# An 18-wide attention beside a recurrent layer: four heads in lockstep, scores in four row tiles, values in four column tiles, division between two 32x32 vector transposes

## The chip, the cores and the metric

The kernel runs on one core of a Trainium2 chip. The metric is the device time of one execution in microseconds (us). The core's engines work side by side, each through its own list of instructions in a fixed order: TensorE (PE; its weight loads are shown apart as PEld), VectorE (DVE), ScalarE (ACT), GpSimd (POOL) and SyncE (SP), which here only issues DMA transfers. The array of TensorE has 128 rows (the contraction) and 128 columns (the outputs). A matmul whose operands use fewer may be placed in a part of the array, a tile of 32 rows or of 32 columns; the place is given in the code as `tile_position`.

## What is computed

Two layers on the same input of 2048 tokens by 576, mixed by a gate per token:

```python
g = _sigmoid((x * gate_w).sum(-1, keepdims=True))
a = _A_ref(x, A_mem0, A_Wq, A_Wk, A_Wv, A_Wo, A_seg_len)
b = _B_ref(x, B_wqkv, B_wo)
return g * a + (1 - g) * b
```

Layer A is recurrent. It goes through 64 segments of 32 tokens; each has 32 heads of 128, its 32 tokens stand behind 8 memory rows (40 positions in all), and the first 8 rows of a segment's output are the memory of the next. Layer B is plain attention over all 2048 tokens with 32 heads that are only 18 wide (`Dh = 576 // 32`):

```python
scores = jnp.einsum('bhqd,bhkd->bhqk', q, k) * scale
p = _softmax(scores, axis=-1)
o = jnp.einsum('bhqk,bhkd->bhqd', p, v)
```

## The kernel before

First x is transposed and layer B's queries, keys and values are projected into DRAM (`qtd`, `ktd`, `vgd`), in 8 groups (`g`) of four heads (`j`); the 18 rows of head j lie at partitions 32j to 32j+17. Then layer A runs, segment by segment. One segment is, on PE: five transposes of the new tokens (`ptx`), the query projection of 160 matmuls of 40 columns (`pb` from `wq`), the value projection of 20 and 20 matmuls of 512 columns (`pvv`) with the 160 of the key projection between them (`pb` from `wk`), the scores (`psh`), the row sums (`psums`), the reciprocal of the sums spread out by a matmul (`psn` from `diag`, which DVE makes), the weighted values (`pso`), the output projection of 160 matmuls of 40 columns (`pbw`) and five transposes (`pto`). Below, "projection stretch" is the time from the end of `pbw` to the first `pb` of `wk`, "key stretch" from there to the first `psums`, and "softmax stretch" from there to the end of `pbw`.

Layer B is cut into steps by the generator `b_steps`, and `b_advance` takes some of them at the end of each segment. A step before is two key blocks of one head: two score matmuls with 18 rows into one tile `sb` of two PSUM banks, one exponential on ACT over both (`etb`, 1024 elements a partition), and two matmuls that add the weighted values into `ob`. `vgd` holds the head's 18 value columns and 18 columns of ones, so that `ob` has the sums of the exponentials in rows 32 to 49. After eight steps DVE takes the reciprocal of those 18 rows, multiplies, and `stage` goes to `otd`. There are 1152 steps, 18 a segment. `sb` has two buffers, `etb` two, `ob` one; `qtg`, `ktg` and `vgi`, a group's operands, have one each, so a new group's load waits for the last use of the old.

The order on each engine is settled when the program is built, by a scheduler that moves instructions between the two layers: a step that is written at the end of segment s is spread over segment s and s+1. Each engine then takes its list strictly in order, and a waiting instruction holds up what is behind it. At the end `fin` multiplies `otd` with the output weights `wop` and mixes both layers.

Of the kernel before, what the change touches and what calls it, by code (L numbers as in the profile page):

```python
# [8 lines left out]
FP32 = mybir.dt.float32  # L9
BF16 = mybir.dt.bfloat16  # L10
ACT = mybir.ActivationFunctionType
ALU = mybir.AluOpType
# [4 lines left out]
def kernel(  # L17
# [15 lines left out]
    nc = tc.nc  # L33
    P = nc.NUM_PARTITIONS

    B_, S, Dm = A_x.shape
# [8 lines left out]
    DhB = Dm // HB  # L45
# [11 lines left out]
    KBB = 2  # L57
# [28 lines left out]
    wop = const.tile([P, GB, Dm], BF16, name="wop")  # L86
# [5 lines left out]
    vgd = dpool.tile([GB, P, NKB * 200], BF16, name="vgd")  # L92
# [5 lines left out]
    def dma(out_ap, in_ap):  # L98
        eng = dma_engs[dma_i[0] % 2]
        dma_i[0] += 1  # L100
        eng.dma_start(out=out_ap, in_=in_ap)

    with ExitStack() as bctx:
# [8 lines left out]
        nc.vector.memset(wop[:], 0.0)  # L112
        wo_v = B_wo.rearrange("(g j e) d -> j e g d", j=4, e=DhB)
        for j in range(4):
            dma(wop[32 * j:32 * j + DhB, :, :], wo_v[j])
# [29 lines left out]
        for g in range(GB):  # L145
# [36 lines left out]
            vg = bwork.tile([P, NKB, 200], BF16, name="vg")  # L182
            nc.vector.memset(vg[:], 0.0)
            nc.vector.memset(vg[:, :, :].rearrange("p k (j e) -> p k j e", e=50)[:, :, :, 32:50], 1.0)
            for kb in range(NKB):
                pv = ps_pj.tile([P, QC], FP32, name="pq")
                for c in range(NC):
                    cz = csz[c]
                    nc.tensor.matmul(
                        pv[:, 0:4 * DhB],  # L190
                        lhsT=xT[0:cz, c, kb * P:(kb + 1) * P],
                        rhs=wvg[0:cz, c, :],
                        start=(c == 0),
                        stop=(c == NC - 1),
                    )
                nc.any.tensor_copy(
                    out=vg[:, kb, :].rearrange("p (j e) -> p j e", e=50)[:, :, 0:DhB],
                    in_=pv[:, 0:4 * DhB].rearrange("p (j e) -> p j e", e=DhB),
                )
# [23 lines left out]
    bint2 = actx.enter_context(tc.tile_pool(name="bint2", bufs=2))  # L223
# [21 lines left out]
    nb_total = [0]  # L245

    def b_steps():
        for g in range(GB):
            qtg = bint.tile([P, S], BF16, name="qtg")
            ktg = bint.tile([P, S], BF16, name="ktg")  # L250
            vg = bint.tile([P, NKB * 200 + P], BF16, name="vgi")
            nc.sync.dma_start(out=qtg[:, :], in_=qtd[g])
            nc.scalar.dma_start(out=ktg[:, :], in_=ktd[g])
            nc.gpsimd.memset(vg[:, NKB * 200:NKB * 200 + P], 0.0)
            nc.sync.dma_start(out=vg[:, 0:NKB * 200], in_=vgd[g])
            for j in range(4):
                for qc in range(NQC):
                    ob = ps_bo.tile([P, 512], FP32, name="ob")
                    for kb0 in range(0, NKB, KBB):
                        nb = min(KBB, NKB - kb0)  # L260
                        sb = ps_bs.tile([P, KBB, 512], FP32, name="sb")
                        for i in range(nb):
                            kb = kb0 + i
                            nc.tensor.matmul(  # L264
                                sb[:, i, 0:QC],
# [6 lines left out]
                        etb = bint2.tile([P, KBB, 512], BF16, name="etb")  # L272
                        nc.scalar.activation(  # L273
                            out=etb[:, 0:nb, 0:QC], in_=sb[:, 0:nb, 0:QC], func=ACT.Exp, scale=scale_b
                        )
                        for i in range(nb):
                            kb = kb0 + i
                            nc.tensor.matmul(  # L278
                                ob[:, 0:QC],
                                lhsT=vg[:, kb * 200 + 50 * j:kb * 200 + 50 * j + P],  # L280
                                rhs=etb[:, i, 0:QC],
                                start=(kb == 0),
                                stop=(kb == NKB - 1),
                            )
                        nb_total[0] += 1
                        yield
                    rtb = bint.tile([P, 512], FP32, name="rtb")
                    nc.vector.reciprocal(out=rtb[0:DhB, 0:QC], in_=ob[32:32 + DhB, 0:QC])  # L288
                    stage = bint.tile([P, 512], BF16, name="stage")
                    nc.gpsimd.memset(stage[32 * j:32 * j + 32, 0:QC], 0.0)  # L290
                    nc.vector.tensor_tensor(
                        out=stage[32 * j:32 * j + DhB, 0:QC],
                        in0=ob[0:DhB, 0:QC],
                        in1=rtb[0:DhB, 0:QC],
                        op=ALU.mult,
                    )
                    nc.sync.dma_start(
                        out=otd[32 * j:32 * j + 32, g, qc * QC:(qc + 1) * QC],
                        in_=stage[32 * j:32 * j + 32, 0:QC],
                    )  # L300
                    yield

# [12 lines left out]

    total_steps = GB * 4 * NQC * ((NKB + KBB - 1) // KBB + 1)

# [198 lines left out]
    ps_f = ctx.enter_context(tc.tile_pool(name="ps_f", bufs=2, space=bass.MemoryType.PSUM))  # L516
    for n in range(NT):
# [33 lines left out]
#: Inputs that are plain numbers.  # L551
# [29 lines left out]
```

## Time and profile before

| | |
|---|---|
| median of 3 runs | 3421.55 us (3415.63 to 3444.35) |
| span of the profiled execution | 3430.3 us |
| PE busy | 3212.1 us, 94% |
| PEld / ACT / DVE / POOL busy | 1838.2 / 1518.2 / 1264.7 / 101.7 us |
| mean granted TensorE clock | 0.865 of full |

The profiled execution has no other time of its own than its span, which is 8.8 us above the median of the three runs. A busy PE in these tables is one with a matmul under way; matmuls overlap, so what a matmul costs is read from the distance between starts, not from its duration. The granted clock is 1.0 (2.4 GHz) or 0.5 (1.2 GHz) at any moment, and a mean of both over a stretch.

### The profile page before, as it was taken

What the parts mean: (1) busy time and instruction counts of PE and PEld (TensorE: products, weight loads), DVE (VectorE), ACT (ScalarE), POOL (GpSimd) and SP (SyncE); (2) the same over time, 40 slices, a digit from 0 to 9 for tenths busy, and PEclk for the clock granted to TensorE, in tenths of its full rate; (3) what the DMA queues carried; (4) which work ended last, traced back from release to release, by engine and by line L of the source; (5) the groups of instructions that cost most, each with busy time, mean ns of one, the idle gap of its engine ahead of it and who ended that gap; (6) DMA issues with size and microseconds to landing.
All of it is one profiled execution on the core that took longest, in us unless ns stands there. A gap on an engine that the chain in (4) does not pass through costs nothing.

```text
span 3430.3 us, 102385 instructions
## 1 busy us (share of the span) xinstructions
PE 3212.1 (94%) x47335; PEld 1838.2 (54%) x47765; DVE 1264.7 (37%) x1771; ACT 1518.2 (44%) x2227; POOL 101.7 (3%) x280
## 2 busy tenths in 40 slices
PE   5799999999999999999999999999999999999996
PEld 3445555555555555555555555555555555555553
DVE  5323433333333333333333433333433334333334
ACT  2334444444444444444444444444444444444440
POOL 0100000000000000000000000000000000000000
PEclk9868898898889888888988888898889888888988
DMA  5640000000000000000000000000000000000004
GB/s 122 191 170 5 4 5 27 4 4 5 5 26 5 5 5 26 5 5 4 5 27 5 4 5 5 26 5 5 5 26 5 5 5 4 27 5 5 5 5 106
DMA packets 92658, 78.36 MB, mean 23 GB/s; under 512 B 65212, under 2 KB 84356, under 8 KB 90500
## 3 DMA queue, kind: packets, MB, share of 16 engines
q1 hardware_dynamic: 62594, 52.33, 5.1%
q10 hardware_dynamic: 29634, 19.46, 2.2%
q8 instruction: 373, 6.11, 0.8%
q14 instruction: 57, 0.47, 0.0%
HBM read 47.90 MB, written 23.86 MB: 21 GB/s over the span
## 4 chain that ended last, share of the span: by engine, by line
PE 87%; issue 6%; DMA 3%; ACT 3%; DVE 1%; ACTq 0%; another core or an unknown queue 0%; DVEq 0%; SPq 0%; POOL 0%; POOLq 0%
PE pb L359 16%; PE pvv L379 16%; PE sb L264 16%; PE ob L278 14%; PE pbw L478 10%; PE psh L401 2%; PE psn L444 2%; PE psh L410 2%; PE pso L462 2%; ACT etb L273 2%; PE psums L425 2%; PE pq L170 1%; DMA ktg<-ktd 1%; PE pto L499 1%; DVE kt_sb L451 1%
## 5 line engine op out<-in xcount | busy, mean ns | idle before, releaser
L273 ACT ACTIVATE etb<-sb 128x1024 bf16<-128x1024 f32 x1024 | 1036.8, 1023 | 550.6 <-PE sb L264 290.5
L264 PE MATMUL sb<-qtg,ktg 18*128 18x512 bf16 x2048 | 710.3, 438 | 44.4 <-issue 17.8
L278 PE MATMUL ob<-etb,vgi 128*128 128x512 bf16 x1730 | 574.9, 405 | 36.3 <-ACT etb L273 18.2
L379 PE MATMUL pvv<-wv,ht 128*128 128x512 bf16 x2463 | 600.3, 380 | 5.4 <-issue 0.2
L288 DVE RECIPROCAL rtb<-ob 18x512 f32<-18x512 f32 x128 | 428.7, 3349 | 312.5 <-PE sb L264 286.9
L387 DVE CAST v_sb<-pvv 40x512 bf16<-40x512 f32 x256 | 174.8, 683 | 657.4 <-PE pvv L379 657.4
L379 PEld LDWEIGHTS <-ht 128*128 128x128 bf16 x2560 | 243.0, 98 | 296.5 <-issue 29.1
L359 PEld LDWEIGHTS <-wq 128*128 128x128 bf16 x10240 | 301.4, 98 | 164.7 <-issue 152.8
L478 PEld LDWEIGHTS <-wo 128*128 128x128 bf16 x10240 | 343.4, 110 | 39.5 <-issue 34.3
L389 ACT CAST v_sb<-pvv 40x512 bf16<-40x512 f32 x256 | 148.3, 579 | 487.3 <-PE pvv L379 487.3
L478 PE MATMUL pbw<-qt_sb,wo 128*128 128x40 bf16 x10240 | 349.6, 194 | 13.7 <-issue 13.6
L359 PE MATMUL pb<-ht,wq 128*128 128x40 bf16 x10240 | 331.4, 184 | 16.8 <-issue 16.4
L264 PEld LDWEIGHTS <-ktg 18*128 18x128 bf16 x2048 | 131.6, 98 | 340.9 <-issue 310.0
L278 PEld LDWEIGHTS <-vgi 128*128 128x128 bf16 x2048 | 156.2, 100 | 249.8 <-issue 198.2
L359 PEld LDWEIGHTS <-wk 128*128 128x128 bf16 x10240 | 268.6, 96 | 15.1
L359 PE MATMUL pb<-ht,wk 128*128 128x40 bf16 x10240 | 269.4, 180 | 0.0
L369 DVE CAST kt_sb<-pb 128x320 bf16<-128x320 f32 x128 | 63.0, 492 | 252.8 <-PE pb L359 252.8
L444 PEld LDWEIGHTS <-ones 40*40 40x40 bf16 x2048 | 81.3, 112 | 133.5 <-issue 125.3
L470 ACT CAST qt_sb<-pso 128x320 bf16<-128x320 f32 x128 | 54.5, 426 | 214.1 <-PE pso L462 214.1
L490 DVE CAST ht<-pbw 128x32 bf16<-128x32 f32 x63 | 12.1, 192 | 330.3 <-PE pbw L478 330.3
L432 DVE RECIPROCAL rq<-psums 40x32 f32<-40x32 f32 x64 | 22.4, 350 | 289.7 <-PE psums L425 289.7
L417 ACT ACTIVATE kt_sb<-psh 40x320 bf16<-40x320 f32 x256 | 110.4, 431 | 39.7 <-PE psh L410 16.1
(81 smaller groups left out, 1897.8 us busy)
## 6 DMA issues: line engine op xcount, KB each, us to landing
vgd<-vg ACTq DMA_DIRECT2D x8, 800.0 KB, 3.8
vgi<-vgd SPq DMA_DIRECT2D x8, 800.0 KB, 5.9
wo<-in_A_Wo_dram SPq DMA_DIRECT2D x1, 4608.0 KB, 54.2
qtd<-stg SPq DMA_DIRECT2D x8, 512.0 KB, 4.0
ktd<-stg SPq DMA_DIRECT2D x8, 512.0 KB, 4.8
qtg<-qtd SPq DMA_DIRECT2D x8, 512.0 KB, 5.1
ktg<-ktd ACTq DMA_DIRECT2D x8, 512.0 KB, 5.2
wq<-in_A_Wq_dram SPq DMA_DIRECT2D x1, 4096.0 KB
```

The costliest lines, as they stand in the source:

```text
L264: nc.tensor.matmul(sb[:, i, 0:QC], lhsT=ktg[32 * j:32 * j + DhB, kb * P:(kb + 1) * P], rhs=qtg[32 * j:32 * j + DhB, qc * QC:(qc + 1) * QC] ...
L273: nc.scalar.activation(out=etb[:, 0:nb, 0:QC], in_=sb[:, 0:nb, 0:QC], func=ACT.Exp, scale=scale_b)
L278: nc.tensor.matmul(ob[:, 0:QC], lhsT=vg[:, kb * 200 + 50 * j:kb * 200 + 50 * j + P], rhs=etb[:, i, 0:QC], start=(kb == 0), stop=(kb == NKB ...
L288: nc.vector.reciprocal(out=rtb[0:DhB, 0:QC], in_=ob[32:32 + DhB, 0:QC])
L359: nc.tensor.matmul(pb[:, 64 * j:64 * j + L], lhsT=w_tile[0:cz, c, h * Dh:(h + 1) * Dh], rhs=ht[0:cz, c, :], start=(c == 0), stop=(c == NC ...
L379: nc.tensor.matmul(ph[:, 0:512], lhsT=ht_flat[0:cz, L * c:L * c + P], rhs=wv[0:cz, c, q8 * qcols:(q8 + 1) * qcols], start=(c == 0), stop=( ...
L387: nc.vector.tensor_copy(out=v_sb[0:L, q8 * qcols:(q8 + 1) * qcols], in_=ph[0:L, :])
L389: nc.scalar.copy(out=v_sb[0:L, q8 * qcols:(q8 + 1) * qcols], in_=ph[0:L, :])
L401: nc.tensor.matmul(psh[0:L, 0:512], lhsT=ident[0:L, 0:L], rhs=mb8[0:L, :], start=True, stop=False,)
L417: nc.scalar.activation(out=vw(et[0:L, HS * h0:HS * (h0 + 8)], HS, L), in_=vw(psh[0:L, :], 64, L), func=ACT.Exp, scale=scale_a,)
L444: nc.tensor.matmul(psn[0:L, 64 * j:64 * j + L], lhsT=ones[0:L, 0:L], rhs=diag3[0:L, L * h:L * (h + 1)], start=True, stop=True,)
L478: nc.tensor.matmul(pbwv[0:cz, c, 0:L], lhsT=wo[:, h, c * P:c * P + cz], rhs=ot_sb[:, HS * h:HS * h + L], start=(h == 0), stop=(h == H - 1),)
```

## The change

Layer B's four heads of a group now go together. A step is one key block of four heads: four score matmuls, one in each 32-row tile of the array, into two `sb` tiles; two exponentials; and four value matmuls with 32 output columns each, one in each 32-column tile of the array, into the four quarters of one `ob`. `vgd` has 32 columns a head: 18 values, one column of ones, 13 of zeros. After sixteen steps DVE turns `ob` over in blocks of 32 by 32, takes the reciprocal of one column per block, multiplies, and turns the result back. There are 512 steps, 8 a segment. `etb` gets a third buffer, the load of `ktg` moves from ACT's queue to SP's, and `wop` is loaded behind layer A instead of at the start.

```diff
-            for j in range(4):
-                for qc in range(NQC):
-                    ob = ps_bo.tile([P, 512], FP32, name="ob")
-                    for kb0 in range(0, NKB, KBB):
...
+            for qc in range(NQC):
+                ob = ps_bo.tile([P, QC], FP32, name="ob")
+                for kb in range(NKB):
+                    sbs = []
+                    for jp in range(2):
+                        sb = ps_bs.tile([P, 2, QC], FP32, name="sb")
+                        for i in range(2):
+                            j = 2 * jp + i
                             nc.tensor.matmul(
-                                sb[:, i, 0:QC],
+                                sb[:, i, :],
                                 lhsT=ktg[32 * j:32 * j + DhB, kb * P:(kb + 1) * P],
                                 rhs=qtg[32 * j:32 * j + DhB, qc * QC:(qc + 1) * QC],
...
                                 tile_position=(32 * j, 0),
                             )
...
-                            nc.tensor.matmul(
-                                ob[:, 0:QC],
-                                lhsT=vg[:, kb * 200 + 50 * j:kb * 200 + 50 * j + P],
-                                rhs=etb[:, i, 0:QC],
...
+                    for j in range(4):
+                        nc.tensor.matmul(
+                            ob[32 * j:32 * j + 32, :],
+                            lhsT=vg[:, kb * P + 32 * j:kb * P + 32 * j + 32],
+                            rhs=ets[j // 2][:, j % 2, :],
...
+                            tile_position=(0, 32 * j),
                         )
...
-                    nc.vector.reciprocal(out=rtb[0:DhB, 0:QC], in_=ob[32:32 + DhB, 0:QC])
...
+                nc.vector.transpose(out=tq[:, :, :].rearrange("p b e -> p (b e)"), in_=ob[:, :])
...
+                nc.vector.reciprocal(out=rtb[:, :, :], in_=tq[:, :, DhB:DhB + 1])
...
+                nc.vector.transpose(out=stage[:, :], in_=tn[:, :, :].rearrange("p b e -> p (b e)"))
```

What the scheduler makes of it on PE in the projection stretch of a segment in mid-run (a line of dots stands for the second instruction of a pair, or for more of the same). Before, two values of one head, two scores of one head, twice over, and then pieces of the query projection:

```order
L278 LDWEIGHTS vgi_22721
L278 MATMUL ob_27910<-etb_27949,vgi_22721 128x512
...
L264 LDWEIGHTS ktg_22720
L264 MATMUL sb_27960<-qtg_22719,ktg_22720 128x512
...
L278 MATMUL ob_27910<-etb_27956,vgi_22721 128x512
...
L264 MATMUL sb_27974<-qtg_22719,ktg_22720 128x512
...
L359 MATMUL pb_28033<-ht_27881,wq_1905 128x40
```

Now, in the same stretch of the same segment:

```order
L270 MATMUL ob_27630<-etb_27667,vgi_22496 32x512
...
L255 LDWEIGHTS ktg_22495
L255 MATMUL sb_27676<-qtg_22494,ktg_22495 128x512
...
L351 LDWEIGHTS wq_1899
L351 MATMUL pb_27739<-ht_27591,wq_1899 128x40
```

The four heads do not stand together: they come as two values, two scores, then 7 to 31 matmuls of the query projection, eight times a segment, then twice two values alone. The stretch opens with three values and four scores in a row. Before, one run of 91 `pb` stood without layer B; now the longest is 31. The 20 `pvv` that were partly mixed with layer B follow in one run.

On PE in the softmax stretch, around the last 8 of the 32 `psn`, before:

```order
L264 MATMUL sb_27925<-qtg_22719,ktg_22720 128x512
L264 MATMUL sb_27932<-qtg_22719,ktg_22720 128x512
...
L444 LDWEIGHTS ones_63
L444 MATMUL psn_27670<-diag3_1946,ones_63 40x40
...
L462 MATMUL pso_27680<-kt_sb_1944,v_sb_1945 128x40
```

Now:

```order
L255 MATMUL sb_27634<-qtg_22494,ktg_22495 128x512
L270 MATMUL ob_27630<-etb_27637,vgi_22496 32x512
L436 MATMUL psn_27380<-diag3_1940,ones_63 40x40
...
L255 MATMUL sb_27645<-qtg_22494,ktg_22495 128x512
L454 MATMUL pso_27390<-kt_sb_1938,v_sb_1939 128x40
...
L454 MATMUL pso_27400<-kt_sb_1938,v_sb_1939 128x40
...
L270 MATMUL ob_27630<-etb_27639,vgi_22496 32x512
```

Where three scores in a row stood ahead of the `psn` and nothing between the 32 `pso`, single scores and values of layer B now stand between pieces of layer A. Over the whole softmax stretch of an even segment the order before was 24 `psums`, 2 scores, 8 `psums`, 2 scores, 2 values, 3 scores, 24 `psn`, 3 scores, 8 `psn`, 32 `pso`, 24 `pbw`, 2 values, 136 `pbw`; it is now 24 `psums`, 2 scores, 8 `psums`, 2 scores, 2 values, 2 scores, 2 values, 1 score, 24 `psn`, 1 score, 8 `psn`, 1 value, 8 `pso`, 1 value, 1 score, 8 `pso`, 2 values, 1 score, 16 `pso`, 16 `pbw`, 2 scores, 1 value, 144 `pbw`. An odd segment differs from it by a few places. In every eighth segment, where a group of heads ends, layer B stands out of the way from the `psn` to the end of `pbw`.

On DVE between `diag` and the memory rows of the next segment (`ht`), before, which stood so once a segment, with a second division in the projection stretch:

```order
L433 TENSOR_TENSOR diag3_1946<-ident_58,rq_1947 40x1280
L288 RECIPROCAL rtb_17529<-ob_16734 18x512
L451 TENSOR_TENSOR kt_sb_1944<-psn_17265,kt_sb_1944 40x320
...
L472 CAST qt_sb_1943<-pso_17315 128x320
L291 TENSOR_TENSOR stage_17531<-ob_16734,rtb_17529 18x512
L472 CAST qt_sb_1943<-pso_17335 128x320
```

Now, in every second segment, and none in the projection stretch:

```order
L425 TENSOR_TENSOR diag3_1940<-ident_58,rq_1941 40x1280
L281 STREAM_TRANSPOSE tq_27621<-ob_25920 128x512
L443 TENSOR_TENSOR kt_sb_1938<-psn_27350,kt_sb_1938 40x320
...
L283 RECIPROCAL rtb_27623<-tq_27621 128x16
L464 CAST qt_sb_1937<-pso_27400 128x320
L285 TENSOR_TENSOR tn_27625<-tq_27621,rtb_27623 128x512
L464 CAST qt_sb_1937<-pso_27420 128x320
L292 STREAM_TRANSPOSE stage_27627<-tn_27625 128x512
```

The first vector transpose has taken the place of the long reciprocal ahead of the four multiplications (`kt_sb` from `psn`) for which PE's `pso` wait; the rest of the division stands behind them.

## Rows read from the trace of the kernel before

**Rows 1.** The page: span, and busy time of each engine.
```profile
span 3430.3 us, 102385 instructions
PE 3212.1 (94%) x47335; PEld 1838.2 (54%) x47765; DVE 1264.7 (37%) x1771; ACT 1518.2 (44%) x2227; POOL 101.7 (3%) x280
```
**Rows 2.** Costliest groups: line, engine, operation xcount | busy us, mean ns | idle before.
```profile
L273 ACT ACTIVATE etb<-sb 128x1024 bf16<-128x1024 f32 x1024 | 1036.8, 1023 | 550.6 <-PE sb L264 290.5
...
L288 DVE RECIPROCAL rtb<-ob 18x512 f32<-18x512 f32 x128 | 428.7, 3349 | 312.5 <-PE sb L264 286.9
```
**Rows 3.** The last instructions of every segment: ns, first and last start in us.
```profile
L499 PEld LDWEIGHTS <-ots x320: 88/96/150, 236.7 to 3373.1; 128*32 128x32 bf16 x128, 64*32 64x32 bf16 x32
```
**Rows 4.** Stretches: limits, length, busy us (instructions), granted clock, DMA share, GB/s.
```profile
2522.45:2544.70 22.25, 21.92 (x237) 9.86 (x240) 7.31 (x11) 13.76 (x17) 0.52 (x1) 1.00 0.03 6
2544.70:2555.60 10.90, 10.85 (x216) 7.34 (x215) 2.35 (x4) 3.86 (x8) 0.33 (x2) 1.00 0.01 2
2506.83:2522.45 15.62, 13.78 (x271) 9.94 (x272) 8.59 (x11) 5.27 (x7) 0.52 (x1) 0.67 0.02 4
1079.00:1102.30 23.30, 22.83 (x237) 10.33 (x239) 7.36 (x11) 13.76 (x17) 0.52 (x1) 0.93 0.03 6
```
**Rows 5.** PE in order of time, projection stretch: start us, us, instruction, count.
```profile
2523.70 0.38 PE L264 MATMUL sb<-qtg,ktg 18*128 18x512 bf16 x1
2523.71 0.26 PE L344 MATMUL ptx<-ident,xseg 32*128 32x32 bf16 x4
...
2525.48 0.59 PE L278 MATMUL ob<-etb,vgi 128*128 128x512 bf16 x2
2526.00 0.60 PE L264 MATMUL sb<-qtg,ktg 18*128 18x512 bf16 x2
2526.53 0.62 PE L359 MATMUL pb<-ht,wq 128*128 128x40 bf16 x18
2527.00 0.59 PE L278 MATMUL ob<-etb,vgi 128*128 128x512 bf16 x2
```
**Rows 6.** The same place of another segment, where the scores work on partitions 0 to 17.
```profile
2575.58 0.60 PE L264 MATMUL sb<-qtg,ktg 18*128 18x512 bf16 x2
2576.02 0.25 PE L344 MATMUL ptx<-ident,xseg 32*128 32x32 bf16 x4
```
**Rows 7.** PE in order of time, first segment, at half clock.
```profile
176.81 1.03 PE L264 MATMUL sb<-qtg,ktg 18*128 18x512 bf16 x2
177.77 1.03 PE L278 MATMUL ob<-etb,vgi 128*128 128x512 bf16 x2
...
188.70 3.21 PE L359 MATMUL pb<-ht,wq 128*128 128x40 bf16 x91
191.74 1.32 PE L278 MATMUL ob<-etb,vgi 128*128 128x512 bf16 x3
```
**Rows 8.** Stretches as in rows 4: around that run, and around a fall.
```profile
175.30:188.70 13.40, 13.01 (x78) 3.59 (x80) 3.52 (x2) 5.12 (x5) 0.00 (x0) 0.50 1.01 425
188.70:192.40 3.70, 3.64 (x93) 3.31 (x94) 1.40 (x3) 0.43 (x1) 0.00 (x0) 0.50 1.01 427
192.40:202.00 9.60, 8.35 (x44) 2.46 (x43) 1.90 (x1) 8.40 (x9) 0.00 (x0) 1.00 1.06 390
1086.60:1090.00 3.40, 3.30 (x65) 1.97 (x66) 3.20 (x1) 1.50 (x3) 0.00 (x0) 1.00 0.00 0
1090.00:1093.50 3.50, 3.28 (x66) 2.38 (x64) 1.81 (x4) 0.84 (x2) 0.00 (x0) 0.51 0.07 16
```
**Rows 9.** PE in order of time, softmax stretch; in brackets the idle time before.
```profile
2514.25 0.42 PE L444 MATMUL psn<-diag,ones 40*40 40x40 bf16 x8 [0.96 <-DVE kt_sb L451]
...
2517.83 4.52 PE L478 MATMUL pbw<-qt_sb,wo 128*128 128x40 bf16 x136 [0.22 <-issue]
```
**Rows 10.** DVE groups as in rows 2, and a transfer with us to landing.
```profile
L387 DVE CAST v_sb<-pvv 40x512 bf16<-40x512 f32 x256 | 174.8, 683 | 657.4 <-PE pvv L379 657.4
...
ktg<-ktd ACTq DMA_DIRECT2D x8, 512.0 KB, 5.2
```

More of the change, by code (lines that the diff above doesn't have):

```diff
@@ L91 @@
     ktd = dpool.tile([GB, P, S], BF16, name="ktd")
-    vgd = dpool.tile([GB, P, NKB * 200], BF16, name="vgd")
+    vgd = dpool.tile([GB, P, NKB * P], BF16, name="vgd")
     otd = dpool.tile([P, GB, S], BF16, name="otd")
@@ L250, in b_steps @@
             ktg = bint.tile([P, S], BF16, name="ktg")
-            vg = bint.tile([P, NKB * 200 + P], BF16, name="vgi")
+            vg = bint.tile([P, NKB * P], BF16, name="vgi")
             nc.sync.dma_start(out=qtg[:, :], in_=qtd[g])
[L253 to L256, printed above, removed]
-                for qc in range(NQC):
-                    ob = ps_bo.tile([P, 512], FP32, name="ob")
-                    for kb0 in range(0, NKB, KBB):
[L260 to L263, printed above, removed]
+            nc.sync.dma_start(out=ktg[:, :], in_=ktd[g])
+            nc.sync.dma_start(out=vg[:, :], in_=vgd[g])
+            for qc in range(NQC):
[6 more added lines that the diff above has]
+                            j = 2 * jp + i
                             nc.tensor.matmul(
-                                sb[:, i, 0:QC],
+                                sb[:, i, :],
                                 lhsT=ktg[32 * j:32 * j + DhB, kb * P:(kb + 1) * P],
@@ L297, in b_steps @@
[L297 to L300, printed above, removed]
-                    yield
+                        sbs.append(sb)
+                    ets = []
+                    for jp in range(2):
+                        etb = bint3.tile([P, 2, QC], BF16, name="etb")
+                        nc.scalar.activation(out=etb[:, :, :], in_=sbs[jp][:, :, :], func=ACT.Exp, scale=scale_b)
+                        ets.append(etb)
@@ new lines, in b_steps @@
+                    for j in range(4):
[3 more added lines that the diff above has]
+                            rhs=ets[j // 2][:, j % 2, :],
+                            start=(kb == 0),
+                            stop=(kb == NKB - 1),
+                            tile_position=(0, 32 * j),
+                        )
+                    yield
+                tq = bint.tile([P, QC // 32, 32], FP32, name="tq")
@@ new lines, in b_steps @@
+                nc.vector.transpose(out=tq[:, :, :].rearrange("p b e -> p (b e)"), in_=ob[:, :])
+                rtb = bint.tile([P, QC // 32, 1], FP32, name="rtb")
+                nc.vector.reciprocal(out=rtb[:, :, :], in_=tq[:, :, DhB:DhB + 1])
+                tn = bint.tile([P, QC // 32, 32], BF16, name="tn")
+                nc.vector.tensor_tensor(
+                    out=tn[:, :, :],
+                    in0=tq[:, :, :],
+                    in1=rtb[:, :, :].to_broadcast([P, QC // 32, 32]),
+                    op=ALU.mult,
+                )
@@ L303 @@
+                stage = bint.tile([P, QC], BF16, name="stage")
+                nc.vector.transpose(out=stage[:, :], in_=tn[:, :, :].rearrange("p b e -> p (b e)"))
+                nc.sync.dma_start(out=otd[:, g, qc * QC:(qc + 1) * QC], in_=stage[:, :])
     bgen = b_steps()
@@ L516 @@
     ps_f = ctx.enter_context(tc.tile_pool(name="ps_f", bufs=2, space=bass.MemoryType.PSUM))
+    finc = ctx.enter_context(tc.tile_pool(name="finc", bufs=1))
+    wop = finc.tile([P, GB, Dm], BF16, name="wop")
+    nc.vector.memset(wop[:], 0.0)
+    wo_v = B_wo.rearrange("(g j e) d -> j e g d", j=4, e=DhB)
+    for j in range(4):
+        dma(wop[32 * j:32 * j + DhB, :, :], wo_v[j])
     for n in range(NT):
```

35 lines of the change are left out of this document (5 added, 30 removed).

## The prediction

> **What bounds the kernel now.** Read the page's busy times first: PE is under way for 94% of the span, no other engine for half of it [rows 1]. The mean segment, from the last instructions of the first to those of the 64th, is (3373.1 - 236.7) / 63 = 49.8 us [rows 3], so 64 segments are nearly the whole span and the change has to be read in one of them. The stretches of one segment say where its time lies: 22.25 us in the projection stretch, 10.90 in the key stretch, 15.62 in the softmax stretch, 48.8 together [rows 4]. In the first two PE is busy to within 0.4 us, ACT for 13.76 of 22.25 us: PE's own list is the bound there, not the exponentials, whose 1024 times 1.02 us [rows 2] are 16.4 us a segment. In the softmax stretch PE has 1.8 us of gaps; 0.96 of them is the wait for a multiplication on DVE [rows 9], ahead of which DVE's list has a 3.35 us reciprocal [rows 2].
>
> The clock is the second thing to see. It is full in the first two stretches and at a mean of 0.67 in the softmax stretch; in another segment it also falls within the projection stretch, which then takes 23.30 us instead of 22.25 [rows 4].
>
> **Prices.** At full clock a pair of scores or of values is 0.53 us from start to start (2525.48, 2526.00, 2526.53), and 18 `pb` take 0.47 us, 0.026 each [rows 5]. At half clock a pair is 0.96 us and 91 `pb` take 3.04 us, 0.033 each [rows 7]. So half clock costs narrow work a quarter, wide work nearly double.
>
> Do tiles overlap? The trace of before has a natural test. The scores of head j use rows 32j to 32j+17, `ptx` uses rows 0 to 31. Where j is not 0, `ptx` starts 0.01 us after a score that takes at least 0.21 us to stream [rows 5]; where j is 0 it starts 0.44 us after the first of two scores [rows 6], when both are through. Two row tiles run at once. A pair in two row tiles then saves one streaming (512 columns: 0.213 us at 2.4 GHz, 0.427 at 1.2), less 0.01 and a little for the loads: I take 0.31 us at full clock and 0.56 at half. The Trainium skill (TensorE: Matmul & The Clock Gate, Part 3) gives 3.07 times for four row tiles; the trace agrees in kind [rows 5, 6]. For column tiles no row of before has two: the bounds are 0.31 (overlap like rows) and 0.53 us (one after the other). I take 0.31, the mechanism being the same array cut the other way, and keep 0.53 as a rival. The same section gives 2.38 times for three column tiles, by which a pair would also come out near the lower bound.
>
> A rule speaks against the change. The row first: two values plus two scores at full clock cost 1.05 us where four streamings make 0.85 [rows 5], so each change of shape costs 0.10 us, and by the same working 0.11 at half clock [rows 7]; going from `pb` to values did not (18 `pb` at 2526.53, values at 2527.00, 0.026 us apiece [rows 5]), and to column tiles it will: ten times 0.10 us in a projection stretch. The Trainium skill (TensorEngine Tiling (Array Packing), Key Properties) states that changing the tiling mode drains the engine; by that rule too the gain is less than the tiles promise.
>
> **The change, part by part.** By the order, four tiles seldom stand together: layer B's 32 scores and 32 values of a segment come as some 35 groups, mostly pairs. That halves the streaming, it does not quarter it.
>
> *Projection stretch, full clock throughout.* 20 groups (three values, four scores, ten pairs of values, eight of scores) at 0.31 = 6.2; 160 `pb` at 0.026 = 4.1; 20 `pvv` at 0.213 = 4.3; ten entries into column tiles 1.0; `pto` and `ptx` 0.8: 16.4 us. Then waits: ten exponentials at 1.03 in a row from 0.9 us on end at 11.5 or so, the last two pairs of values wait for them, and behind stand 16 to 22 `pb` and the `pvv`: about 0.9 us more, 17.3 in all, against 22.25.
>
> *Projection stretch at half clock* from 2.5 us after its start: 2.5 + 17 groups at 0.56 (9.5) + 160 `pb` at 0.033 (5.3) + ten entries at 0.11 (1.1) + `pvv`. In the first segment the clock came back at 192.40, after 3.7 us of the unbroken run of `pb` and values from 188.70 [rows 7, 8]; so I let some eleven `pvv` (4.7 us) run at 0.427 and nine at 0.213: 6.6. Sum 25.0 us.
>
> *Key stretch:* nothing of layer B in it before or now, 10.9.
>
> *Softmax stretch.* Before, 10 scores and 4 values stood in it; now 12 and 9, in 14 groups, half of them single, which save nothing, and mostly at half clock. Going down the new list from the first `psums`: last 8 `psums` at 1.0, first pair of values at 2.2 (it waits for its exponential), second at 3.25, `psn` at 4.4, last 8 `psn` at 5.8, `pso` from 6.8 to 10.5, 16 `pbw`, two scores, one value, 144 `pbw` from 12.4 at 0.033 to 17.1. Against 15.62 that loses 1.5 us, although the 0.96 us behind the reciprocal are gone.
>
> *DVE.* Two divisions a segment, each 3.35 us of reciprocal [rows 2] and more, become one per two segments of two transposes, a 16-element reciprocal and a multiplication. No row has a transpose; the bounds are 0.68 us (a cast of 512 from PSUM [rows 10]) and 3.35 (the 512-element reciprocal [rows 2]). I take 0.68. It is then over before the first `psn` is through, and costs nothing; at 3.35 it would put about 2 us before the `pso` of every second segment, 64 us over the run. I keep 64 for the upper end.
>
> *The rest.* ACT: the same 1024 exponentials. `ktg` on SP's queue stands behind `qtg`, 5.2 us to land [rows 10]; it is due while 160 `pbw` (5 us) and 32 `psn` and `pso` run, so it costs nothing, 5 us for each of seven groups if that cover went. `wop` behind layer A waits for a memset and a load like that, beside the first `otn`: about 4 us at the end. It removes as little at the start.
>
> **Sum.** A segment is 17.3 + 10.9 + 17.1 = 45.3 us where the clock holds in the projection stretch and 25.0 + 10.9 + 17.1 = 53.0 where it does not. The mean now is 49.8. So all hangs on the share of segments in which it falls; at 4.5 / 7.7 = 0.58 of them nothing is gained.
>
> What did PE do when it fell? Between 1086.60 and 1090.00 PE was busy 3.30 of 3.40 us, with 18-row scores and `pb`, hardly any value matmul, and the clock was at half right after [rows 8]. From 175.30 to 188.70 it stayed at half with PE busy 13.01 of 13.40 us on alternating pairs with 8 to 23 `pb` between [rows 8]. So a busy PE does not hold the clock; work that fills little of the array lets it go, and short pieces do not fetch it back. The change does just this: values fill 64 columns at a time instead of 128, no run of `pb` exceeds 31, and the first 2 us of the projection stretch hold seven tile matmuls, the ten small transposes and a wait. At the other end the `pbw`, in which the clock came back, are cut by two scores and a value. Against it: in mid-stretch `pb` now stand in every gap, 40 full columns each 0.026 us, which held the clock in the key stretch's 160. I cannot work a share out of rows. I take 0.48, one segment in two: 45.3 + 0.48 x 7.7 = 49.0 us, 0.8 less than now, 64 times: -51 us, +4 at the end. From the span, 3430.3 - 47 = 3383; the span is 8.8 above the median of the runs, so about 3375.
>
> **Rivals.**
> *The clock holds* in all but 0.15 of the segments: 46.5 us, 64 x -3.3 = -211 + 4, from the median 3214. For it: the steady `pb`. The Trainium skill's page (TensorE: Matmul & The Clock Gate, Why this matters for your kernels) asks only that PE not stand idle; by that rule this rival would be what comes, for PE has no long gap; the trace bears that out badly [rows 8].
> *The clock is lost* in 0.9 of them: 52.2 us, 64 x 2.4 = +154 + 4, 3580: slower. It decides from 0.58 on. For it: PE's work around the fall and in the long half-clock stretch [rows 8].
> *Column tiles take turns:* 11 groups of values cost 0.22 more at full clock or 0.42 at half in the projection stretch, three pairs 0.4 in the softmax stretch: +4.8 us a segment on the likeliest, 53.8: 64 x 4.0 = +256 + 4, 3682. For it: no row shows column tiles together. Against: row tiles do overlap [rows 5, 6].
>
> **Chances.** About half the segments 0.37, with its own range of 3300 to 3470; clock held 0.20; clock lost 0.30; columns in turn 0.13. The range leaves out the lower half of the second and the upper part of the last two, with the transposes' bound of 64 us in it: 3210 to 3680. Within 1% (3387 to 3456) is about what a measurement of this kernel cannot tell from no change. Faster: 0.20 and half of the first case, 0.39. Same: about a third of the first and a little of the third, 0.15. Slower: the rest, 0.46.
>
> **What will show it.** Two scores of a pair, and two values, should start within 0.02 us of each other; if values start 0.21 apart, columns take turns. A pair at full clock should cost 0.31 us. The stretches of several segments should be 17 us at clock 1.0 or 25 near 0.5, and the share of each is the test of the sum. The softmax stretch should be longer than before, some 17 us. The transposes should be near 0.7 us and no `pso` wait for them. I am wrong in the mechanism if the projection stretch at full clock exceeds 19 us: then ACT or a wait bounds it.

## The result, and the profile after

The changed kernel takes 3174.55 us (median of 4 runs, 3170.39 to 3178.94) against 3422.87 us of the kernel before, beside which it ran: ratio 0.927, 95% interval 0.924 to 0.930. It is 7.3% faster. The prediction had said 3375 us, in a range from 3210 to 3680, with 0.39 for faster; the time lies below the range, nearest to the rival "the clock holds" (3214).

The page of the changed kernel, with the rows that answer to [rows 1] and [rows 2] (L267 is the exponential, L281 and L292 are the two transposes, L283 the reciprocal between them, L285 the multiplication):

```profile
span 3176.8 us, 101992 instructions
PE 3024.0 (95%) x47622; PEld 1807.9 (57%) x47765; DVE 813.6 (26%) x1664; ACT 1481.7 (47%) x2206; POOL 33.7 (1%) x144
...
L267 ACT ACTIVATE etb<-sb 128x1024 bf16<-128x1024 f32 x1024 | 1011.0, 1024 | 385.2 <-PE sb L255 370.3
```

From its groups by line, DVE's share of layer B:

```profile
L281 DVE STREAM_TRANSPOSE tq<-ob 128x512 f32<-128x512 f32 x32 | 22.9, 717 | 14.9 <-PE ob L270 14.9
L292 DVE STREAM_TRANSPOSE stage<-tn 128x512 bf16<-128x512 bf16 x32 | 22.5, 703 | 0.3
L285 DVE TENSOR_TENSOR tn<-tq,rtb 128x512 bf16<-128x512 f32 x32 | 21.8, 682 | 0.0
```

PE is still under way for 95% of a shorter span; DVE lost a third of its work: the divisions took 428.7 us of long reciprocals [rows 2] and 86.8 us of multiplications over the run, and the new ones take 75 us in all. A transpose costs 0.70 to 0.72 us.

The last instructions of every segment, as in [rows 3], give a mean segment of (3115.1 - 236.9) / 63 = 45.7 us instead of 49.8:

```profile
L491 PEld LDWEIGHTS <-ots x320: 88/96/97, 236.9 to 3115.1; 128*32 128x32 bf16 x128, 64*32 64x32 bf16 x32
```

63 x 4.1 = 258 us: the gain is all in the segments. In the mean over 63 segments, from the records of the trace, the projection stretch went from 22.9 to 18.5 us, the key stretch stayed at 11.0 and the softmax stretch went from 16.0 to 16.3. The clock has no part in this gain: over the span its mean fell from 0.865 to 0.826, and in the projection stretch from 0.97 to 0.92. What the tiles save by overlapping is more than what the clock takes back.

Stretches as in [rows 4] (projection, key and softmax stretch of a segment in mid-run, then the projection stretch behind the start of a group of heads, and two pieces of the softmax stretch ahead of that one):

```profile
2334.61:2351.68 17.07, 16.63 (x235) 9.23 (x234) 3.26 (x9) 11.15 (x15) 0.00 (x0) 1.00 0.03 8
2351.68:2362.60 10.92, 10.87 (x216) 7.36 (x215) 2.35 (x4) 3.86 (x8) 0.33 (x2) 1.00 0.01 2
2318.47:2334.55 16.08, 15.36 (x280) 9.99 (x277) 4.58 (x8) 7.10 (x9) 0.00 (x0) 0.68 0.01 2
2374.65:2403.16 28.51, 27.45 (x248) 11.47 (x247) 3.27 (x9) 15.67 (x19) 0.00 (x0) 0.58 0.01 4
2362.00:2366.30 4.30, 3.26 (x62) 2.00 (x59) 1.96 (x3) 2.80 (x4) 0.00 (x0) 1.00 0.21 62
2366.30:2373.00 6.70, 6.24 (x174) 5.91 (x171) 4.60 (x10) 0.85 (x2) 0.00 (x0) 0.50 0.59 217
```

A projection stretch with the clock held is 17.07 us, as predicted (17.3), and one that loses it, behind the start of a group, 28.51 here. But of 63 segments 50 hold the clock there and only 13 lose it: 7 in which the matmuls of a new group of heads stand, and 6 others. PE in order of time shows the pairs, at full clock in the first four rows and at half clock in the last three (as in [rows 5] and [rows 7]):

```profile
2336.51 0.39 PE L270 MATMUL ob<-etb,vgi 128*32 128x512 bf16 x2 [0.21 <-ACT etb L267]
2336.83 0.39 PE L255 MATMUL sb<-qtg,ktg 18*128 18x512 bf16 x2
2337.15 0.37 PE L351 MATMUL pb<-ht,wq 128*128 128x40 bf16 x8
2337.45 0.39 PE L270 MATMUL ob<-etb,vgi 128*32 128x512 bf16 x2
...
2384.66 0.61 PE L270 MATMUL ob<-etb,vgi 128*32 128x512 bf16 x2
2385.20 0.61 PE L255 MATMUL sb<-qtg,ktg 18*128 18x512 bf16 x2
2385.74 1.21 PE L351 MATMUL pb<-ht,wq 128*128 128x40 bf16 x31
```

Two values take 0.32 us from start to start (2336.51 to 2336.83) and two scores 0.32 (to 2337.15); at half clock 0.54. Both kinds of tile overlap.

### The profile page after: what moved, and what is told of

Read it like the earlier page. It is cut to its first block, busy times and chain, and to the rows that moved or that the text cites. A ratio compares the mean times of both kernels' runs of the same rounds, so it can differ in the third digit from the quotient of the medians.

```text
span 3176.8 us, 101992 instructions
## 1 busy us (share of the span) xinstructions
PE 3024.0 (95%) x47622; PEld 1807.9 (57%) x47765; DVE 813.6 (26%) x1664; ACT 1481.7 (47%) x2206; POOL 33.7 (1%) x144
## 4 chain that ended last, share of the span: by engine, by line
PE 88%; ACT 6%; DMA 3%; DVE 1%; issue 1%; ACTq 0%; SPq 0%; DVEq 0%
PE pb L351 19%; PE pvv L371 18%; PE ob L270 13%; PE sb L255 13%; PE pbw L470 11%; ACT etb L267 5%; PE pso L454 3%; PE psh L393 3%; PE psn L436 3%; PE psh L402 2%; PE pq L164 2%; PE psums L417 1%; DMA otn<-otd 1%; DMA wq<-in_A_Wq_dram 1%; PE po L525 1%
## 5 line engine op out<-in xcount | busy, mean ns | idle before, releaser
L267 ACT ACTIVATE etb<-sb 128x1024 bf16<-128x1024 f32 x1024 | 1011.0, 1024 | 385.2 <-PE sb L255 370.3
L270 PE MATMUL ob<-etb,vgi 128*32 128x512 bf16 x2048 | 527.3, 471 | 55.0 <-ACT etb L267 49.4
L255 PE MATMUL sb<-qtg,ktg 18*128 18x512 bf16 x2048 | 537.4, 465 | 0.0
L351 PE MATMUL pb<-ht,wq 128*128 128x40 bf16 x10240 | 382.2, 185 | 15.4 <-DMA wq<-in_A_Wq_dram 15.4
L255 PEld LDWEIGHTS <-ktg 18*128 18x128 bf16 x2048 | 106.9, 94 | 264.7 <-issue 255.7
L361 DVE CAST qt_sb<-pb 128x320 bf16<-128x320 f32 x128 | 62.9, 492 | 623.2 <-PE pb L351 617.4
L270 PEld LDWEIGHTS <-vgi 128*32 128x32 bf16 x2048 | 121.6, 95 | 168.9 <-issue 122.8
L443 DVE TENSOR_TENSOR kt_sb<-psn,kt_sb 40x320 bf16<-40x320 f32 x256 | 111.8, 475 | 73.1 <-PE psn L436 72.6
L454 PEld LDWEIGHTS <-v_sb 40*128 40x128 bf16 x2048 | 79.8, 107 | 75.9 <-issue 75.0
L363 ACT CAST kt_sb<-pb 128x320 bf16<-128x320 f32 x128 | 54.4, 425 | 129.9 <-PE pb L351 129.9
```

Of the source, the lines that this page charges most:

```text
L255: nc.tensor.matmul(sb[:, i, :], lhsT=ktg[32 * j:32 * j + DhB, kb * P:(kb + 1) * P], rhs=qtg[32 * j:32 * j + DhB, qc * QC:(qc + 1) * QC], s ...
L267: nc.scalar.activation(out=etb[:, :, :], in_=sbs[jp][:, :, :], func=ACT.Exp, scale=scale_b)
L270: nc.tensor.matmul(ob[32 * j:32 * j + 32, :], lhsT=vg[:, kb * P + 32 * j:kb * P + 32 * j + 32], rhs=ets[j // 2][:, j % 2, :], start=(kb == 0),
L351: nc.tensor.matmul(pb[:, 64 * j:64 * j + L], lhsT=w_tile[0:cz, c, h * Dh:(h + 1) * Dh], rhs=ht[0:cz, c, :], start=(c == 0), stop=(c == NC ...
L361: nc.vector.tensor_copy(out=dst, in_=src)
L443: nc.vector.tensor_tensor(out=vw(et[0:L, HS * h0:HS * (h0 + 8)], HS, L), in0=vw(psn[0:L, :], 64, L), in1=vw(et[0:L, HS * h0:HS * (h0 + 8)] ...
```

## The experiments

Theory A: the gain is the overlap of the tiles; without it the clock would be lost as well, because it falls where a busy PE works with little of its array. Theory B: the clock falls only where PE waits, and the gain is DVE's long reciprocals or the new order. In the table, "lost" counts the segments, of 63, whose mean granted clock between the output transposes and the first `pvv` is below 0.95, from the records of the trace; the mean segment is worked out as above.

| kernel | us | ratio to before (95%) | mean segment | lost |
|---|---|---|---|---|
| before | 3423 | 1 | 49.8 | 21, most for a few us alone |
| changed | 3175 | 0.927 (0.924-0.930) | 45.7 | 13 |
| no overlap | 4094 | 1.198 (1.190-1.206) | 60.2 | 57 |
| column tiles alone overlap | 3794 | 1.107 (1.104-1.110) | 55.2 | 44 |
| row tiles alone overlap, values full width | 3260 | 0.952 (0.950-0.954) | 47.0 | 9 |
| query projection with 64 rows | 3486 | 1.021 (1.015-1.026) | 50.5 | 63 |
| scores over 32 rows | 3142 | 0.919 (0.915-0.923) | 45.0 | 8 |
| early loads | 3191 | 0.932 (0.927-0.937) | 45.8 | 16 |
| 32 rows and early loads | 3101 | 0.906 (0.904-0.907) | 44.4 | 1 |
| the same, wide softmax | 2981 | 0.870 (0.868-0.872) | 42.6 | 1 |
| before, no long reciprocal | 3373 | 0.985 (0.983-0.987) | 49.1 | 6 |

### Overlap undone

```
-    j = 2 * jp + i              # a pair: two heads, one key block
+    j = 2 * jh + jp; kb = 2 * kp + i   # a pair: one head, two key blocks
-    for j in range(4): value(head j, kb)
+    for jp, i in ((0, 0), (0, 1), (1, 0), (1, 1)): value(head 2*jh + jp, block 2*kp + i)
```

> The changed kernel with one thing undone: the two score matmuls of a pair belong to the same head and so to the same row tile, and the two value matmuls of a pair to the same column tile, so nothing overlaps inside TensorE. Transposes, division, loads and the number of matmuls stay. Theory A (the gain is the overlap of the tiles): a pair goes back from 0.32 to 0.53 us at full clock; 8 steps of 4 pairs a segment make 32 x 0.21 = 6.7 us, so about 3175 + 63 x 6.7 = 3600 us, more if more segments lose the clock. Theory B (the gain is the long reciprocals gone from VectorE, and the order of the work): about 3175 us.

Measured 4094 us, 20% slower than before, with the same matmuls and transposes as the changed kernel. PE in order of time, in a segment that holds the clock and in one that does not:

```profile
1855.64 0.61 PE L274 MATMUL ob<-etb,vgi 128*32 128x512 bf16 x2
1856.17 0.60 PE L257 MATMUL sb<-qtg,ktg 18*128 18x512 bf16 x2
1856.71 0.52 PE L355 MATMUL pb<-ht,wq 128*128 128x40 bf16 x14
...
2271.86 1.04 PE L274 MATMUL ob<-etb,vgi 128*32 128x512 bf16 x2
2272.83 1.03 PE L257 MATMUL sb<-qtg,ktg 18*128 18x512 bf16 x2
2273.79 0.58 PE L355 MATMUL pb<-ht,wq 128*128 128x40 bf16 x12
```

The pair is back at 0.53 us, as expected, which is worth 32 x 0.21 x 63 = 423 us. The expected 3600 us fell short by the other 500, which go with the clock: 57 segments lose it, and a pair is then 0.97. Theory B's 3175 is out: the new division is in this kernel too. Its list of work is not quite the changed kernel's, since the scheduler set it anew; another list alone moved the count of lost segments from 13 to 16 (early loads, below), not to 57. The changed kernel without overlap is what the prediction feared: narrow tiles that let the clock go.

### One overlap at a time

Row tiles' overlap alone is undone by the scores of the last experiment with the values in their former order over heads:

```
-    for jp, i in ((0, 0), (0, 1), (1, 0), (1, 1)):
+    for jp, i in ((0, 0), (1, 0), (0, 1), (1, 1)):   # two heads next to each other: two column tiles
```

> Row tiles' overlap undone alone: the two scores of a pair belong to one head and take turns, the value pairs still go to two column tiles and overlap; each step takes two heads and two key blocks. The score pairs cost 16 x 0.21 = 3.4 us more a segment at full clock. If each of the two overlaps carries its own share: 3175 + 214 = 3390 us. Theory A adds that matmuls of 18 rows one at a time leave the array emptier for longer, so that most segments lose the clock: another 8 us in each of some 40 segments, 3700 us, and with the value pairs overlapped below the 4094 us of no overlap at all.

Column tiles' overlap alone is undone by value weights of 128 columns:

```
-    ob[32 * j:32 * j + 32, :], lhsT=vg[:, kb * P + 32 * j:kb * P + 32 * j + 32],
-    start=(kb == 0), stop=(kb == NKB - 1), tile_position=(0, 32 * j),
+    ob[:, :], lhsT=vg[:, kb, PJ[j] - 32 * j:PJ[j] - 32 * j + P],   # zeros outside the head's 32
+    start=(kb == 0 and j == 0), stop=(kb == NKB - 1 and j == 3),
```

> The changed kernel without its column tiles: each value matmul has weights of all 128 columns, zeros outside its head's 32, and the four heads add up in one accumulation; the score pairs still overlap. The value pairs take turns again, 0.53 instead of 0.32 us: 16 x 0.21 = 3.4 us a segment. Theory A (array at work decides): the value matmuls now work with the whole array, so the clock holds in nearly all segments, the 6 irregular ones too: 3175 + 63 x 3.4 - 6 x 4.7 = 3360 us. Theory C (the clock falls because the stretch between the full-size matmuls is long, whatever fills it): the projection stretch is as long as where pairs don't overlap, most segments lose the clock, 25 us instead of 16.6 + 3.4: 3700 us or more.

Measured 3794 and 3260 us. Both give back one overlap of the two, 16 pairs a segment, so by streaming alone they should be alike. With full-width values the clock holds in 54 of 63 segments: PE in order of time shows values 0.54 apart, two scores 0.32, and the stretch from the output transposes to the first `pvv` is at full clock although it is 15.62 us long instead of 11.8:

```profile
1972.19 0.60 PE L277 MATMUL ob<-etb,vgi 128*128 128x512 bf16 x2
1972.73 0.39 PE L262 MATMUL sb<-qtg,ktg 18*128 18x512 bf16 x2
1973.05 0.61 PE L277 MATMUL ob<-etb,vgi 128*128 128x512 bf16 x2
```

```profile
1924.77:1940.39 15.62, 15.32 (x218) 7.78 (x216) 1.72 (x5) 12.17 (x14) 0.00 (x0) 1.00 0.02 6
```

With 18-row scores one after the other 44 segments lose the clock; in one of them the same stretch is 24.19 us long, at 0.53, and PE has no gap at all in it:

```profile
2117.24:2141.43 24.19, 24.19 (x213) 9.04 (x213) 1.73 (x5) 11.03 (x12) 0.00 (x0) 0.53 0.02 4
```

There a pair of scores takes 0.96 us from the first one on that follows the small transposes, 1.5 us into the stretch. So the length of the stretch does not decide (theory C is out); what fills it does. Row tiles are the larger part of the change: without them 619 us are lost, without column tiles 85. The two prices do not add up on their own: with the rows' overlap gone, taking the columns' away too costs 300 us more (4094), because the clock goes with it.

The expectation for full width was 100 us too high. The softmax stretch became 1.5 us shorter (16.3 to 14.8 in the mean), and not by the clock, whose mean there is 0.64 against 0.63: the new list left some 17 of layer B's matmuls in it instead of 23. The projection stretch took the others in and is still no longer than expected (21.3 us); why isn't accounted for. Nor does this run say by what the full-width values hold the clock, as they are wider and also take longer, 0.54 us a pair instead of 0.32.

### The query projection with half of its rows

```
-    cz = csz[c]
+    cz = 64 if engsel == 0 else csz[c]     # the query projection contracts 64 rows
```

> The changed kernel with the query projection contracting 64 of the 128 rows of each chunk (half of that contraction is left out): the same number of matmuls of the same 40 columns, with half of the array's rows at work. Theory A (the clock falls where TensorE, though busy, works with a small part of its array): the 50 segments that hold the clock in the projection stretch lose it, 16.6 becomes up to 25.5 us, so 3400 to 3600 us. Theory B (the clock falls only where TensorE waits): no more waits than before, so 3175 us within 1%.

Measured 3486 us, as theory A expected, with 63 of 63 segments lost. PE in order of time at a fall:

```profile
2047.62 0.37 PE L351 MATMUL pb<-ht,wq 64*128 64x40 bf16 x8
2047.91 0.39 PE L270 MATMUL ob<-etb,vgi 128*32 128x512 bf16 x2
2048.24 0.39 PE L255 MATMUL sb<-qtg,ktg 18*128 18x512 bf16 x2
2048.56 1.07 PE L351 MATMUL pb<-ht,wq 64*128 64x40 bf16 x31
2049.55 0.61 PE L270 MATMUL ob<-etb,vgi 128*32 128x512 bf16 x2
2050.10 0.60 PE L255 MATMUL sb<-qtg,ktg 18*128 18x512 bf16 x2
```

No gap is in these rows; the pairs go from 0.32 to 0.54 us. With 128 rows the same list (PE's weight loads stand in the same order, one by one) holds the clock in 50 segments. So the rows of the `pb` in the gaps between pairs decide in the changed kernel. The Trainium skill (TensorE: Matmul & The Clock Gate, Why this matters for your kernels) asks for no idle gap of PE against a drop of the clock; here it drops without one, so that rule is not enough.

### Scores over 32 rows, early loads, and both

```
-    lhsT=ktg[32 * j:32 * j + DhB, ...], rhs=qtg[32 * j:32 * j + DhB, ...]
+    lhsT=ktg[32 * j:32 * j + 32, ...],  rhs=qtg[32 * j:32 * j + 32, ...]     # rows 18 to 31 are zeros
```

> The changed kernel with the scores contracting all 32 rows of a row tile (14 of them zeros on both sides, so that the sums are the same) instead of 18. Theory A (part of the array at work decides): the 6 segments outside the starts of a group that lose the clock (21.5 to 22.9 us instead of 16.6) keep it, about 6 x 5.5 = 33 us less: 3140 us; the 7 segments at the starts of a group stay as they are. Theory B (only waits decide): no change, 3175 us.

Measured 3142 us, as expected, again with the changed kernel's list: the six falls outside the starts of a group are gone, the seven at the starts stand (and the first segment now loses the clock too). For the clock the rows of zeros counted like others, and they cost no time: in the probe below 160 scores over four tiles took 8.74 us with 32 rows as with 18.

```
+    # in query block 2 of group g: queries and keys of group g + 1 into a second buffer
+    # in the last query block, behind key blocks 3, 7, 11, 15: a quarter of the values of g + 1
```

> The changed kernel with the queries, keys and values of the next group of heads loaded ahead: a second buffer for queries and keys, the values in four pieces that are each refilled when their last use is over. Expected by theory A: the 7 segments in which a group ends no longer run their softmax stretch without the other layer's matmuls, and hold the clock afterwards: projection stretch 28.5 to 16.6 us, softmax stretch 12.3 to 16.1, so 7 x 8 = 57 us less, 3118 us. If the clock falls there for another reason (VectorE's division at the end of a query block): 3165 to 3175 us.

Measured 3191 us, no gain. The softmax stretches without layer B and the 28 us projection stretches behind them are gone, as expected. But only four of the seven segments then hold the clock; three lose it as ordinary segments do (22.9 us), and so do others: 16 in all. The scheduler set other lists, and with 18-row scores a segment of the usual kind is so near to the fall that small differences decide. That is a reading of the counts; the next run tests it.

> Both edits on the changed kernel: the scores contract 32 rows (zeros in 14 of them) and the next group's loads are issued ahead. Theory A (the clock falls where little of the array is at work): no segment but the first ones loses the clock; a group's last two segments go from 55.6 + 40.3 us (scores over 32 rows alone) to 2 x 44.5, 7 x 6.9 = 48 us less than 3142: 3094 us. If the early loads cost elsewhere, as they did without the 32 rows: 3140 to 3160 us.

Measured 3101 us: only the first segment loses the clock, and the early loads, worth nothing by themselves, bring 1.4 points here (ratio 0.919 to 0.906). The expectation was 3094. This kernel and the last have the same list on PE, weight load by weight load, so that the 14 rows of zeros alone take the lost segments from 16 to 1 and the time from 3191 to 3101 us.

### The softmax stretch over the whole array

```
-    psh[0:L, 64*j:64*j + L], lhsT=kt_sb[:, HS*h:HS*h + L]
+    psh[:, 64*j:64*j + L],   lhsT=kt_sb[:, HS*h:HS*h + P]     # likewise mask, psums, psn
-    lhsT=v_sb[0:L, ...], rhs=et[0:L, ...]
+    lhsT=v_sb[:, ...],   rhs=et[:, ...]                        # v_sb is zero below row L
```

> The kernel with 32 rows and early loads, and in the softmax stretch the recurrent layer's matmuls (mask, scores, sums, normalisers, outputs) use all 128 rows and columns of the array instead of 40, with zeros where a sum must not change and results in the other partitions that nobody reads. The number of matmuls and of streamed columns stays. Theory A (array at work decides): the clock, 0.60 to 0.74 in the stretch from the mask matmul to the transposes of the output, holds there too; 20 us become about 15, the segment 39.4, 2790 us. Theory B (waits of TensorE decide): the stretch waits as before, 3100 us. In between if the waits for ScalarE and VectorE still make it fall in part.

Measured 2981 us, the fastest here, 13% below the kernel before. From the mask matmul ahead of the scores to the output transposes, first with 40 rows and columns, then over the whole array:

```profile
1860.01:1880.53 20.52, 20.18 (x321) 11.69 (x320) 6.93 (x14) 9.51 (x16) 0.33 (x2) 0.67 0.03 9
```

```profile
1741.71:1759.44 17.73, 16.98 (x322) 10.96 (x321) 4.77 (x11) 9.03 (x16) 0.33 (x2) 0.81 0.01 2
```

Theory A gets its sign, at no cost in instructions, but not its size: 120 us of the 310 expected, and at most half of that goes with the clock. In the mean the segment is 1.8 us shorter. Of that 0.9 us lie in the softmax stretch (16.7 to 15.9), where the mean clock rose from 0.64 to 0.72. The other 0.9 lie in the key stretch (10.96 to 10.04), at full clock in both kernels. There each quarter of the scores, from one mask matmul to the next, went from 0.62 to 0.42 us, first with 40 rows and columns, then over the whole array:

```profile
1860.02 0.39 PE L410 MATMUL psh<-mb,ident 40*40 40x512 bf16 x1
...
1860.64 0.39 PE L410 MATMUL psh<-mb,ident 40*40 40x512 bf16 x1
...
1741.93 0.38 PE L417 MATMUL psh<-mb,ident 128*128 128x512 bf16 x1
...
1742.35 0.38 PE L417 MATMUL psh<-mb,ident 128*128 128x512 bf16 x1
```

Mask and scores had two shapes, 40 x 40 and 128 x 40, and now have one: two changes of shape less a quarter, and 0.20 us is the prediction's price for two. That this is the cause was not tried by itself. The clock still falls, later. I took it to hold throughout; layer B's single scores and values and the one-column `psums` still stand in this stretch, and whether they are what drops it was not tried.

### DVE's part by itself

```
-    nc.vector.reciprocal(out=rtb[0:DhB, 0:QC], in_=ob[32:32 + DhB, 0:QC])
+    nc.vector.tensor_copy(out=rtb[0:DhB, 0:QC], in_=ob[32:32 + DhB, 0:QC])
```

> The kernel before with the reciprocal of 512 elements replaced by a copy (the division is left out, all else stays): VectorE's part of the change by itself. Theory A: VectorE is waited for about 1 us a segment at most, so 3350 to 3420 us. Theory B (the long reciprocals were what the change got rid of): 3175 to 3250 us.

Measured 3373 us, 1.5% below before (interval 1.3 to 1.7%). 3.35 us became 0.68:

```profile
L288 DVE COPY rtb<-ob 18x512 f32<-18x512 f32 x128 | 87.3, 682 | 273.5 <-PE ob L278 270.8
```

That is some 50 us (0.7 in the mean segment, 49.8 to 49.1), against the change's 248: a fifth. It is measured in the kernel before; in the changed one DVE's part may differ.

### Each kind of matmul by itself

> No part of the reference is computed: stretches of one kind of matmul each, back to back, no waits, each stretch behind 110 full-size matmuls (128 rows, 128 columns, 512 streamed). Theory A expects the granted clock to fall in stretches that use little of the array, although TensorE never waits (18 rows one tile after the other; 32 columns one tile alone), and to hold where more of it is used (four row tiles or four column tiles in turn, full-size matmuls of 40 streamed columns); in the last stretch, scores and values in turn as in the changed kernel, it expects it to hold or to fall late. Theory B (only waits decide) expects full clock in every stretch. Pairs of tiles: 0.32 us at full clock as in the changed kernel, single ones 0.27 us each.

Stretches of the probe: limits, length, PE busy (instructions), granted clock, DMA share, GB/s. In order: 18 rows one tile, until the clock fell and from there on; 18 rows, four tiles in turn; 32 columns, four tiles in turn; 128 rows by 40 streamed columns; 64 rows by 40, from the fall on; four scores and four values alternating.

```profile
30.05:35.60 5.55, 5.55 (x27) 1.00 0.00 0
35.60:58.87 23.27, 23.27 (x56) 0.50 0.00 0
84.72:93.46 8.74, 8.74 (x161) 1.00 0.02 4
191.12:202.02 10.90, 10.90 (x201) 1.00 0.01 3
225.56:244.12 18.56, 18.16 (x702) 1.00 0.02 4
271.15:290.36 19.21, 19.21 (x580) 0.50 0.02 4
316.51:336.20 19.69, 19.69 (x241) 1.00 0.01 2
```

And 32 columns of all rows, one tile alone (PE, PEld, DVE and POOL busy, then as above):

```profile
149.90:167.27 17.37, 17.37 (x81) 7.68 (x80) 0.00 (x0) 0.00 (x0) 1.00 0.00 1
```

PE is busy for the whole of the second and the sixth stretch, in which the clock is at half: theory B is out for good. 18 rows alone and 64 rows lose the clock; 128 rows by 40 columns hold it. One expectation missed: 32 columns alone kept it through 17.37 us. So theory A holds for matmuls with few rows; for few columns no run here shows it by itself. In the last stretch 18-row scores and 32-column values, four tiles at a time, hold the clock without any `pb`.

Four tiles in turn overlap fully: 160 scores in 8.74 us are 0.055 each, against 0.216 from start to start one at a time (expected: 0.27). In the last stretch eight matmuls of two shapes take 19.69 / 30 = 0.66 us where streaming at 0.055 each would make 0.44, which leaves 0.11 for a change of shape. With it the kernel's pairs add up: 0.22 + 0.11 = 0.33 for a pair of tiles, where 0.32 was measured, and 2 x 0.216 + 0.11 = 0.54 for a pair that takes turns, where it was 0.53.

## Why the prediction was wrong

**What failed: the share of segments that lose the clock.** The prediction took 0.48, said that it could not work it out of rows, and let all hang on it. It was 13 of 63, 0.21. By its own price, 7.7 us a segment, that is 0.27 x 7.7 x 63 = 131 us of the 208 by which the segments came out shorter ((49.0 - 45.7) x 63). The first half of its reading of the falls was right: a busy PE does not hold the clock (query projection with 64 rows, the probe). What was wrong was the conclusion, "The change does just this". One of its reasons was that values fill 64 columns at a time instead of 128; in the probe values of 32 columns by themselves kept full clock, and it was 18 rows, one tile at a time, that lost it. And it did not weigh enough that two overlapping tiles use their parts of the array at once and leave the time in half, so that the `pb` follow sooner. The runs that take the overlap away show how much it is: from 13 lost segments to 44 and 57. The counter-argument the prediction gave, 40 full columns in every gap, was the one to follow, and the 64-row run shows that the rows of those `pb` decide.

**Mis-sized: the softmax stretch.** 17.1 us foretold, 16.3 in the mean of 63 segments (16.08 in the stretch shown), 52 us over the run. The list had been taken mostly at half clock, but it begins at full clock, and the first pairs run at 0.32 us before the fall: in the stretch shown the `psn` start 3.9 us after the first `psums` instead of 4.4. The other half of the 1.0 us lies behind them. PE in order of time:

```profile
2320.66 0.39 PE L270 MATMUL ob<-etb,vgi 128*32 128x512 bf16 x2 [0.52 <-ACT etb L267]
2320.98 0.39 PE L255 MATMUL sb<-qtg,ktg 18*128 18x512 bf16 x2
2321.57 0.39 PE L270 MATMUL ob<-etb,vgi 128*32 128x512 bf16 x2 [0.20 <-ACT etb L267]
...
2322.40 0.99 PE L436 MATMUL psn<-diag,ones 40*40 40x40 bf16 x24
2323.32 0.60 PE L255 MATMUL sb<-qtg,ktg 18*128 18x512 bf16 x1
```

**Right.** A pair is 0.32 us (foretold 0.31) at full clock and 0.54 (0.56) at half; column tiles overlap as row tiles do, so "take turns" falls. A change of shape costs 0.11 us in the probe (0.10). The projection stretch is 17.07 us held (17.3) and the key stretch 10.92 (10.9). The 50 held projection stretches have a mean of 16.6 us, the first three, which hold little of layer B, among them. The transposes cost 0.72 and 0.70 us (0.68), near the lower bound, and no `pso` waits for them. At the end `wop` costs PE's first `po` a wait of 11.78 us where it was 7.14, about the 4 us foretold; before and now:

```profile
3380.49 5.51 PE L527 MATMUL po<-wop,otn 128*128 128x64 bf16 x31 [7.14 <-DMA otn<-otd]
...
3127.08 0.64 PE L525 MATMUL po<-wop,otn 128*128 128x512 bf16 x2 [11.78 <-DMA wop<-in_B_wo_dram]
```

**Right by luck.** The 13 lost projection stretches have a mean of 25.5 us, where 25.0 was foretold, but none of them is that long. The seven behind the start of a group of heads take 28.5 us, and the prediction has no term for them; the six others take 22.0, so that a usual fall costs some 5 us and not 7.7.

**The rivals.** "The clock holds" was nearest, at a share of 0.15; it had 0.20. "The clock is lost" is what the kernel without overlap does. DVE's part, for which the prediction allowed the 0.96 us of one wait a segment [rows 9], measured 0.7 in the kernel before.

**Open.** How rows and columns count against each other isn't settled: 64 of 128 rows lost the clock where 32 of 128 columns kept it, but the two streamed 40 and 512 columns. The values and scores of the kernel stand in pairs; the probe gives 0.055 us a matmul where four stand together, against 0.16 in a pair. An order in fours was not tried. The third buffer of `etb`, the moved loads and the new list were not undone by themselves; the kernel without overlap has the first two and is slower than before.

## What to carry to other kernels

Price a narrow matmul twice: its own time, and what it does to the clock of all that stands around it. Where work uses few rows, put it on tiles that overlap, widen it with zeros where that costs no time (32 rows instead of 18, 128 instead of 40), and keep full-row matmuls between. Where a forecast hangs on a share that no row gives, measure the stretch by itself or make the range reach to both ends of it.

## What the runs showed of the hardware

- The granted clock fell to half with PE busy for every bit of the stretch: 18 rows one tile at a time (23.27 of 23.27 us at 0.50), 64 rows by 40 columns (19.21 of 19.21 us at 0.50).
- Rows of zeros counted as work: scores over 32 rows, 14 of them zeros, ended six falls and saved 32 us with the same list on PE, and 90 us with the list of the early loads (16 lost segments to 1).
- Four row tiles, and four column tiles, overlap fourfold in a steady run (0.0546 and 0.0545 us each against 0.216 and 0.217 one at a time). The Trainium skill (TensorE: Matmul & The Clock Gate, Part 3) gives 3.07 for four row tiles; here it is 4.0.
- A 32x32 block transpose of 128x512 on DVE took 0.717 us from PSUM in 32 bits and 0.703 us from SBUF in 16 bits, a cast of 40x512 from PSUM 0.683 [rows 10].
